# Block-sparse attention with a gated feed-forward: the second batch's value sums taken head couple by head couple, and another order of the opening

## The chip, the cores and the metric

The program runs on one core of one Trainium2 chip. The metric is the device time of one execution in microseconds (us), the median of several. The core has five engines that follow queues of their own and meet at semaphores: PE (matrix products, with PEld, its weight loads, beside it), DVE (vector operations), ACT (activations and copies), POOL (elementwise work on SBUF) and SP, which only issues DMAs.

## The reference, cut to what matters

Four batches of 8 heads, 768 positions, head size 64. Each position attends to its neighbours at a distance under 16 and to 24 summaries of blocks of 32 keys; the result feeds two large products with a piecewise gate between them.

```python
k_sum = k.reshape(B, H, nb, block, D).max(axis=3)
v_sum = v.reshape(B, H, nb, block, D).mean(axis=3)
scores_l = scale * np.matmul(q, k.transpose(0, 1, 3, 2))      # kept where |i-j| < 16
scores_s = scale * np.einsum('bhsd,bhnd->bhsn', q, k_sum) + np.log(block)
a = softmax(concat(masked scores_l, scores_s))
x = np.matmul(a, concat(v, v_sum))                            # (B*S, H*D)
h = x @ w_in
g = np.where(h >= 1, h, np.where(h <= -1, 0.0, (h + 1) ** 2 / 4))
out = g @ w_out
```

## The kernel before

The 3072 positions are worked in eight chunks `c` of 384, two to a batch, and the heads of a chunk in four couples `p`, 128 partitions each. Every piece of work is a **step**, named by a letter and its indices in hexadecimal; a step issues all its instructions on one engine, and the dictionary `steps` names its function.

Attention of a couple, with its engine: `r` load the raw keys, `k` and `q` load windowed keys and queries, `y` load the raw values, `v` load the value windows (all SP); `R` block maxima of keys (DVE), `K`, `C` put windows and maxima in place (POOL); `S` scores (PE), `M` mask and row maximum (DVE), `E` exponentials, `i` a guard on the sums (ACT), `D` reciprocals (DVE), `N0`, `N1` normalise the two heads (POOL), `T0`, `T1` transpose them (PE), `P0`, `P1` copy them out (ACT, or DVE where `P_DVE` lists them). For the value sums: `Y` sums blocks of 32 values (DVE, L256) into the tile `vsum`, `Z` transposes the sums on PE into `vs_ps` (L273 or L275), `V` scales them by 1/32 on ACT into `mean`, `W` spreads `mean` over the rows of the value tile (POOL, L284). `A` is the product with the values (PE, L358), `X` and `L` split its result into a high and a low part.

The feed-forward: `F` c f k is a quarter of the first product (three matmuls into the tile `h`), `G H I J O` the gate and the split of its result (ACT, ACT, DVE, ACT, POOL), `B` c f nine matmuls of the second product into `acc`; `U` copies `acc` to an output tile and `o` stores it. The weights come in sixteen pairs of 1 MB: `w` loads pair i (even ones of `w_in`, odd ones of `w_out`), `a`, `b` scale its words (ACT), `c` i 0 to 5 join them (DVE), `d` rounds to the high half (POOL where `HI_POOL` lists the pair, else ACT), `e` takes the rest (POOL, L186).

Order. `OPENING` is a table of 544 steps for chunk 0, most of the attention of chunk 1, all conversions of weights and the start of the feed-forward of chunk 1; in it every engine runs its steps in the order of the table. After it only PE's order is written by hand: for each chunk `c` from 1 a loop over sixteen `f` does two columns of `F` with their gates, `meet` does `A X L` of one couple of the next chunk and starts the next couple through its scores and norms, `turn` finishes a couple up to its transposes, and then come the `B` of two columns before. The other engines get those steps in an order that a scheduler sets at build time. For chunk 2, the first of batch 1, `y20`..`y23` and `Y20`..`Y23` stand at the end of the opening, and `turn(2, 0)` runs one `Z20 V20` for all four couples: one transpose of the whole `vsum` tile, 128 x 128. Chunk 0 does it couple by couple.

Raw keys, raw values, joined weights and output tiles share three buffers (tag `w` of the pool `stage`, `W_BUFS = 3`): a load into one waits until the tile that had it three allocations before is read or stored.

```python
    def turn(c, p):
        s = f"{c}{p}"
        if c % NHALF == 0 and p == 0:
            do(f"Z{s} V{s}")
        do(f"W{s} T{s}0 P{s}0 T{s}1 P{s}1")
...
        do(OPENING)
        do(" ".join(f"y{NHALF}{p} Y{NHALF}{p}" for p in range(NPAIR)))
```

Of the kernel before, what the change touches and what calls it, by code (L numbers as in the profile page):

```python
# [40 lines left out]
OPENING = """
r00 R00 K00 C00 q00 S00 m h M00 E000 E001 i00 y00 r03 R03 r01 q03 w0 g r02 K03 C03 K01 Y00 R01 q01 D00 a0 b0 S03 Z00
M03 R02 v00 V00 w2 y01 C01 N000 T000 P000 N001 T001 P001 c01 c00 y03 E031 S01 q02 W00 K02 E030 i03 c02 M01 A00 X00
D03 c03 c04 c05 N030 T030 v03 v01 a2 C02 N031 E010 E011 k10 w1 P030 Y03 T031 L00 Z03 S02 d0 e0 q10 Y01 y02 n i01
P031 M02 b2 Z01 c20 v02 k12 w4 V03 V01 E021 C10 E020 D01 W03 q12 w8 w3 F000 w6 F010 N010 N011 A03 c22 T010 k11 X03
W01 c21 c23 c24 i02 T011 S10 D02 L03 c25 P010 N021 Y02 t N020 M10 T021 P011 b1 a1 A01 w5 k13 q11 v10 Z02 P021 V02
X01 L01 c10 w7 w9 c11 T020 P020 d2 W02 A02 E100 X02 c12 L02 c14 b4 a4 C12 e2 F011 F001 F002 F003 c13 c15 d1 e1 F012
F013 c41 c40 G00 H00 S12 I00 c42 q20 wa wd k20 wc G01 H01 wb I01 r20 F030 F031 F020 F021 E101 J00 F032 i10 O00 c44
c43 J01 b3 F022 F033 D10 c45 O01 N101 a3 F023 B00 M12 d4 N100 e4 G03 G02 c30 c31 c32 c33 c34 c35 H03 b6 T100 B01 H02
P100 a6 I03 I02 F050 c60 a5 J02 b5 c61 d3 e3 c62 c63 F040 J03 a8 b8 F051 c64 F041 c50 c65 c51 F052 F042 F053 F043  # L50
O02 O03 B02 c52 d6 e6 T101 G04 H04 c53 c54 a7 I04 G05 J04 H05 B03 E121 c55 c80 I05 c82 P101 b7 c81 F070 F060 c84 J05
d5 c83 F071 c70 b9 aa F061 F072 O04 e5 F062 c85 c72 c71 c74 c73 c75 F073 F063 G06 ba C11 W10 O05 H06 B04 S11 G07 I06
M11 d8 e8 A10 d7 H07 I07 ca0 ca2 ca1 ca4 E120 B05 F090 F080 F091 ca3 J07 bc i12 D12 F081 J06 ca5 a9 e7 O06 F092 ac
O07 F082 X10 c90 L10 F093 F083 G09 da B06 G08 N120 H08 H09 c92 c91 I09 I08 c93 ea N121 E111 c94 c95 ab T120 cc0 cc2
cc1 cc4 B07 q13 F0b0 F0a0 J09 P120 F0b1 J08 cc3 cc5 d9 we wf F0a1 E110 bb F0b2 F0a2 O09 F0b3 F0a3 T121 O08 e9 v13
v12 W12 G0b i11 cb0 D11 N110 dc ec P121 B08 T110 cb2 cb4 cb1 cb3 af G0a H0b A12 B09 H0a be R20 I0a cb5 P110 ae I0b
db eb F0c0 F0d0 ce1 F0c1 F0d1 F0c2 F0d2 F0c3 X12 bf ad L12 ce0 ce2 J0a O0a ce4 ce3 ce5 F0d3 J0b O0b C13 N111 bd B0a
v11 G0d de T111 W11 cd0 cd2 G0c H0c cd1 H0d cd3 P111 ee cd4 cd5 B0b A11 S13 I0c I0d M13 J0d cf0 cf1 cf3 cf2 dd C20
ed F0e0 F0f0 F0e1 J0c O0c O0d E131 E130 cf4 F0f1 F0e2 F0f2 F0e3 G0e i13 B0c F0f3 D13 N131 W13 N130 H0e I0e J0e O0e
F110 B0d cf5 G0f H0f X11 L11 I0f T130 F100 F111 F101 T131 F102 df ef J0f P130 B0e P131 A13 X13 O0f L13 B0f U01 U02  # L60
o02 o01 U00 o00 F112 F103 F113
"""
# [16 lines left out]
def fused_kernel(ctx: ExitStack, tc: tile.TileContext, q2, kT, kwin, vT, vwin, w_in, w_out, mask, ident, out):
# [187 lines left out]
    def turn_vals(c, p):  # L267


        if f"{c}{p}" not in HALF:  # L270
            vs_pss[c, p] = ps.tile([P, 512], F32, tag="ps", name=f"vs_ps{c}_{p}")
        if c == 0:
            nc.tensor.transpose(vs_pss[c, p][:NSUM, P:2 * P], vsum[:, p, :NSUM], ident_sb)  # L273
        else:
            nc.tensor.transpose(vs_pss[c, p][:, :P], vsum.rearrange("p a b -> p (a b)"), ident_sb)  # L275
# [70 lines left out]
    def turned(c, p, j):  # L346
        pts[c, p, j] = att.tile([P, T], F32, tag=f"pt{j}", name=f"pt{c}_{p}_{j}", bufs=1)
        if f"{c}{p}{j}" in P_DVE:
            nc.vector.tensor_copy(out=pts[c, p, j][:KA], in_=t_pss[c, p, j][:KA, :T])
# [259 lines left out]
```

## Time and profile before

| what | value |
|---|---|
| median of 3 runs (lowest to highest) | 648.8 us (647.68 to 649.06) |
| the profiled execution: its own time, its span | 648.22 us, 646.4 us |
| mean granted PE clock | 0.995 |
| busy: PE, PEld, DVE, ACT, POOL | 621.3, 551.8, 244.5, 357.0, 267.8 us |
| DMA read, written | 65.00 MB, 6.29 MB |

The span runs from the first to the last instruction; 1.8 us of the time lie around it. A timeline row gives start, length, engine, line, operation and tiles, how many instructions are merged in it, and in brackets the idle time of the engine before it with what ended it. Matmuls are pipelined, so their printed lengths overlap; what a run of them takes is read from start to start.

### The profile page before, as it was taken

The numbers are of one execution on the slowest core, as the hardware profiler recorded it, in microseconds if no ns is written. First come the engines' busy times: TensorE is split into PE (matmuls) and PEld (weight loads), VectorE is DVE, ScalarE is ACT, GpSimd is POOL, SyncE is SP. The second block draws the span as 40 slices with busy tenths as digits, with TensorE's granted clock in tenths as the row PEclk, the third lists the DMA queues.
The fourth block names the chain that finished last, engine by engine and source line by source line (L and its number), as shares of the span: only waits on it lengthen the run. The fifth ranks groups of instructions, "written<-read, shape, count | busy, mean of one in ns | idle before, by whom it ended". The sixth has DMA issues, their size and how long they took to land.

```text
span 646.4 us, 11580 instructions
## 1 busy us (share of the span) xinstructions
PE 621.3 (96%) x4423; PEld 551.8 (85%) x4423; DVE 244.5 (38%) x462; ACT 357.0 (55%) x953; POOL 267.8 (41%) x307
## 2 busy tenths in 40 slices
PE   3899999599999999999999999999999999999997
PEld 2678988588989988988998898899889899889996
DVE  6999985532224322241223522143222222221111
ACT  4999984545446545545545554564554555443332
POOL 3889996252333333243334233334423333322221
PEclk9999999899999999999999999999999999999999
DMA  9999602822206322240223620152222110000001
GB/s 332 412 414 410 237 26 78 273 86 73 69 12 210 97 74 73 73 167 29 73 73 114 202 71 29 46 194 73 73 73 68 61 44 19 2 17 33 1 1 49
DMA packets 28167, 72.04 MB, mean 111 GB/s; under 512 B 2800, under 2 KB 3056, under 8 KB 28112
## 3 DMA queue, kind: packets, MB, share of 16 engines
q1 hardware_dynamic: 28112, 71.30, 31.3%
q8 instruction: 35, 0.57, 0.4%
q14 instruction: 20, 0.16, 0.1%
HBM read 65.00 MB, written 6.29 MB: 110 GB/s over the span
## 4 chain that ended last, share of the span: by engine, by line
PE 92%; DMA 3%; ACT 1%; POOL 1%; DVE 1%; SPq 1%; issue 0%; POOLq 0%
PE h L395 41%; PE acc L436 41%; PE o_ps L358 4%; PE s_ps L300 3%; PE t_ps L344 3%; DMA raw<-in_w_in 1%; DMA vraw<-in_vT 1%; DVE c L150 0%; POOL halves L186 0%; ACT pt L351 0%; ACT raw L142 0%; ACT raw L132 0%; DVE vsum L256 0%; POOL e L339 0%; SPq L209 0%
## 5 line engine op out<-in xcount | busy, mean ns | idle before, releaser
L395 PE MATMUL h<-xhi,halves 128*128 128x384 f32 x1024 | 276.2, 340 | 2.2 <-DVE t L413 1.7
L436 PE MATMUL acc<-halves,ghi 128*128 128x512 f32 x768 | 237.9, 391 | 0.0
L423 POOL TENSOR_TENSOR glo<-t,ghi 128x384 fp32r<-128x384 f32 x128 | 129.4, 1016 | 208.7 <-PE acc L436 190.6
L395 PEld LDWEIGHTS h<-xhi,halves 128*128 128x128 f32 x1024 | 186.4, 188 | 8.9 <-issue 3.6
L395 PE MATMUL h<-xlo,halves 128*128 128x384 f32 x512 | 172.4, 337 | 0.1
L436 PEld LDWEIGHTS acc<-halves,ghi 128*128 128x128 f32 x768 | 144.7, 189 | 28.6
L436 PE MATMUL acc<-halves,glo 128*128 128x512 f32 x384 | 153.5, 400 | 0.0
L413 DVE SCALAR_TENSOR_TENSOR t<-h,t 128x384 f32<-128x384 f32 x128 | 71.0, 557 | 213.9 <-ACT t L407 211.9
L401 ACT ACTIVATE t<-h,small 128x384 f32<-128x384 f32 x128 | 73.3, 574 | 87.8 <-PE h L395 87.1
L326 ACT ACTIVATE e<-e,den 128x120 f32<-128x120 f32 x192 | 73.3, 383 | 57.9 <-DVE den L315 57.9
L395 PEld LDWEIGHTS h<-xlo,halves 128*128 128x128 f32 x512 | 96.5, 189 | 1.7 <-DVE xlo L381 0.4
L418 ACT CAST ghi<-t 128x384 fp32r<-128x384 f32 x128 | 65.1, 511 | 58.7 <-DVE t L413 39.2
L436 PEld LDWEIGHTS acc<-halves,glo 128*128 128x128 f32 x384 | 72.4, 189 | 13.4 <-POOL glo L423 0.6
L407 ACT ACTIVATE t<-t 128x384 f32<-128x384 f32 x128 | 66.6, 524 | 2.1
L339 POOL TENSOR_TENSOR e<-e,den 128x360 f32<-128x360 f32 x64 | 49.5, 790 | 43.9 <-DVE den L335 43.2
L284 POOL COPY v<-mean 24x768 f32<-24x768 f32 x30 | 24.7, 823 | 78.9 <-DMA v<-in_vwin 54.5
L381 DVE TENSOR_TENSOR xlo<-o_ps,xhi 128x384 fp32r<-128x384 f32 x32 | 17.8, 555 | 86.5 <-ACT xhi L376 86.4
L376 ACT CAST xhi<-o_ps 128x384 fp32r<-128x384 f32 x30 | 14.4, 480 | 60.4 <-PE o_ps L358 60.4
L186 POOL TENSOR_TENSOR halves<-w,halves 128x1024 fp32r<-128x1024 f32 x16 | 38.6, 2418 | 0.6
L326 ACT ACTIVATION_READ_ACCUMULATOR e<-e,den 128x1 f32 x192 | 35.9, 187 | 0.0
L358 PEld LDWEIGHTS o_ps<-pt,v 120*64 120x64 f32 x720 | 24.0, 140 | 10.3 <-issue 8.8
L311 DVE SCALAR_TENSOR_TENSOR e<-s_ps,mask_sb 128x360 f32<-128x360 f32 x64 | 30.9, 524 | 4.8 <-PE s_ps L300 4.8
(61 smaller groups left out, 402.7 us busy)
## 6 DMA issues: line engine op xcount, KB each, us to landing
v<-in_vwin SPq DMA_DIRECT2D x29, 384.0 KB, 3.2
q<-in_q SPq DMA_DIRECT2D x28, 384.0 KB, 4.4
k<-in_kwin SPq DMA_DIRECT2D x28, 360.0 KB, 4.9
raw<-in_w_in SPq DMA_DIRECT2D x8, 1024.0 KB, 10.0
raw<-in_w_out SPq DMA_DIRECT2D x8, 1024.0 KB, 13.2
out<-o SPq DMA_DIRECT2D x24, 256.0 KB, 2.1
kraw<-in_kT SPq DMA_DIRECT2D x13, 384.0 KB, 3.8
vraw<-in_vT SPq DMA_DIRECT2D x13, 384.0 KB, 3.9
```

Source lines behind the costliest of these rows:

```text
L186: nc.gpsimd.tensor_tensor(out=lo, in0=converting[i].bitcast(F32), in1=hi.bitcast(F32), op=ALU.subtract)
L311: nc.vector.scalar_tensor_tensor(out=e, in0=es[c, p, j], scalar=1.0 / math.sqrt(D), in1=mask_sb[:, at:at + NT], op0=ALU.mult, op1=ALU.add)
L326: nc.scalar.activation(out=es[c, p, j][:, t, :], in_=s[:, t, :], func=AF.Exp, bias=nm[:, t:t + 1], scale=scale, accum_out=den[:, t:t + 1])
L339: nc.gpsimd.tensor_tensor(out=e, in0=e, in1=den.unsqueeze(2).broadcast_to([P, NT, KA]), op=ALU.mult)
L358: nc.tensor.matmul(o_pss[c, p][j * D:(j + 1) * D, cols], v_ts[c, p][:KA, blk, j * D:(j + 1) * D], pts[c, p, j][:KA, cols], start=True, sto ...
L395: nc.tensor.matmul(hs[c, f][:, :T], w[:, k], x, start=(k == 0 and n == 0), stop=(k == NK - 1 and n == len(products) - 1))
L401: nc.scalar.activation(out=ts[c, f], in_=hs[c, f][:, :T], func=AF.Relu, bias=ones_half, scale=0.5)
L407: nc.scalar.square(out=ts[c, f], in_=ts[c, f])
L413: nc.vector.scalar_tensor_tensor(out=g, in0=hs[c, f][:, :T], scalar=1.0, in1=ts[c, f], op0=ALU.max, op1=ALU.min)
L418: nc.scalar.copy(out=hi, in_=ts[c, f])
L423: nc.gpsimd.tensor_tensor(out=lo, in0=ts[c, f], in1=hi.bitcast(F32), op=ALU.subtract)
L436: nc.tensor.matmul(acc[c][i], a[:, rows], w, start=(f == 0 and n == 0), stop=(f == NF - 1 and n == len(products) - 1))
```

## The change

The opening's 544 steps stay the same set and get another order, a few of them another engine. Among much else, `S11`, which stood behind `B04`, now stands with `S12` ahead of the `F` steps of the second weight pair; the conversion of pair 4 starts ahead of that of pair 1 and of pair 2; and the couples of chunk 0 come in the order 0, 1, 2, 3 instead of 0, 3, 1, 2. The sums of batch 1's values (chunk 2) are no longer issued at the opening's end: `y2p`, `Y2p` come with the couple they belong to, and each couple has its own `Z2p V2p`, on 24 columns instead of the whole tile.

```diff
 OPENING = """
-r00 R00 K00 C00 q00 S00 m h M00 E000 E001 i00 y00 r03 R03 r01 q03 w0 g r02 K03 C03 K01 Y00 R01 q01 D00 a0 b0 S03 Z00
...
+r00 R00 K00 C00 q00 r01 R01 S00 m h M00 E001 E000 K01 g C01 q01 r03 i00 w0 y00 r02 K03 S01 b0 a0 R03 q02 M01 D00
...
-P_DVE = "130".split()
-X_DVE = "10 11".split()
+P_DVE = "110 120 121 131".split()
+X_DVE = "11 13".split()
...
-HI_POOL = [0, 1, 2, 3, 4, 5, 6, 8, 10, 11, 12, 13]
+HI_POOL = [0, 1, 2, 3, 4, 5, 6, 8, 9, 10, 14, 15]
...
     def turn_vals(c, p):
...
-        if c == 0:
+        if c <= NHALF:
             nc.tensor.transpose(vs_pss[c, p][:NSUM, P:2 * P], vsum[:, p, :NSUM], ident_sb)
...
     def mean_vals(c, p):
-        if c == 0:
+        if c <= NHALF:
             nc.scalar.mul(out=mean[p * SB:p * SB + NSUM], in_=vs_pss[c, p][:NSUM, P:2 * P], mul=1.0 / SB)
...
     def heads(c, p):
...
-                f"v{s} ")
+                f"y{s} v{s} Y{s} " if c == NHALF else f"v{s} ")
...
     def turn(c, p):
...
-        if c % NHALF == 0 and p == 0:
+        if c == NHALF or c % NHALF == 0 and p == 0:
             do(f"Z{s} V{s}")
...
         do(OPENING)
-        do(" ".join(f"y{NHALF}{p} Y{NHALF}{p}" for p in range(NPAIR)))
```

What this does to the queues is shown at three places. First SP, where the opening ends. Before, its rows from the stores of chunk 0's output (`out<-o_2`, and so on) to the raw values of the four couples (`vraw_0` to `vraw_3`, the steps `y20` to `y23`) and the first raw keys of that batch (`kraw_1`):

```order
L448 DMA out<-o_2_1450 128x512
L448 DMA out<-o_1_1448 128x512
L448 DMA out<-o_0_1454 128x512
L220 DMA q_2_1786<-in_q 128x768
L228 DMA vraw_0_1466<-in_vT 128x768
L228 DMA vraw_1_1469<-in_vT 128x768
L228 DMA vraw_2_1472<-in_vT 128x768
L215 DMA k_3_1975<-in_kwin 128x720
L228 DMA vraw_3_1475<-in_vT 128x768
L209 DMA kraw_1_1588<-in_kT 128x768
```

The same place on SP in the changed kernel:

```order
L448 DMA out<-o_2_1459 128x512
L448 DMA out<-o_0_1461 128x512
L448 DMA out<-o_1_1457 128x512
L220 DMA q_2_1783<-in_q 128x768
L228 DMA vraw_0_1500<-in_vT 128x768
L209 DMA kraw_1_1579<-in_kT 128x768
L228 DMA vraw_1_1656<-in_vT 128x768
L215 DMA k_3_1978<-in_kwin 128x720
L209 DMA kraw_2_1779<-in_kT 128x768
L228 DMA vraw_2_1853<-in_vT 128x768
L209 DMA kraw_3_1976<-in_kT 128x768
L228 DMA vraw_3_2050<-in_vT 128x768
```

The first couple's raw values keep their place behind the stores; the others now alternate with the raw keys, and the store of `o_1`, whose buffer `vraw_0` takes over, is the last of the three instead of the second.

Second DVE, at the sums themselves (`vsum<-vraw_p` is `Y2p`, `ksum<-kraw_p` is `R2p`, `den` the reciprocals `D20`, `t_1` to `t_3` the gates `I11` to `I13`). Before:

```order
L413 SCALAR_TENSOR_TENSOR t_1_1522<-h_1_1359,t_1_1522 128x384
L256 TENSOR_REDUCE vsum<-vraw_0_1466 128x24
L335 RECIPROCAL den_0_1495<-den_0_1495 128x6
L256 TENSOR_REDUCE vsum<-vraw_1_1469 128x24
L413 SCALAR_TENSOR_TENSOR t_2_1543<-h_2_1530,t_2_1543 128x384
L256 TENSOR_REDUCE vsum<-vraw_2_1472 128x24
L413 SCALAR_TENSOR_TENSOR t_3_1564<-h_3_1551,t_3_1564 128x384
L256 TENSOR_REDUCE vsum<-vraw_3_1475 128x24
L248 TENSOR_REDUCE ksum<-kraw_1_1588 128x24
```

The same place in the changed kernel:

```order
L413 SCALAR_TENSOR_TENSOR t_1_1513<-h_1_1360,t_1_1513 128x384
L256 TENSOR_REDUCE vsum<-vraw_0_1500 128x24
L335 RECIPROCAL den_0_1483<-den_0_1483 128x6
L248 TENSOR_REDUCE ksum<-kraw_1_1579 128x24
L413 SCALAR_TENSOR_TENSOR t_2_1534<-h_2_1521,t_2_1534 128x384
L413 SCALAR_TENSOR_TENSOR t_3_1555<-h_3_1542,t_3_1555 128x384
L256 TENSOR_REDUCE vsum<-vraw_1_1656 128x24
L248 TENSOR_REDUCE ksum<-kraw_2_1779 128x24
L256 TENSOR_REDUCE vsum<-vraw_2_1853 128x24
```

`Y20` keeps its place, with the reciprocals `D20` right behind it; `Y21` and the later sums stand behind the gates now, and PE's `Z20` waits for `Y20` alone.

Third DVE at the end of its conversions, from the last joins of weight pair 15 (`w_1320<-raw`, the step `cf5`). Before:

```order
L165 ISA w_1320<-raw_1050,c_0_1288 128x1024
L335 RECIPROCAL den_3_1278<-den_3_1278 128x6
L413 SCALAR_TENSOR_TENSOR t_14_1334<-h_14_1298,t_14_1334 128x384
L165 ISA w_1320<-raw_1050,c_1_1290 128x1024
L374 CAST xhi_1_1376<-o_ps_1_1249 128x384
```

The same place in the changed kernel:

```order
L349 COPY pt_1_0_1316<-t_ps_1_0_1237 120x384
L165 ISA w_1320<-raw_1170,c_0_1296 128x1024
L153 SCALAR_TENSOR_TENSOR c_1_1298<-raw_1170,c_1_1298 128x512
L165 ISA w_1320<-raw_1170,c_1_1298 128x1024
L413 SCALAR_TENSOR_TENSOR t_14_1343<-h_14_1284,t_14_1343 128x384
```

The gate `I0e` (`t_14`) stood ahead of the last join and now stands behind it. Ahead of that join DVE now has three copies `P110`, `P120`, `P121` more, and `X10` and `I0e` less. On POOL the step `df` of this pair is new, and it stands behind `O0e` there, the rest of the gate whose minimum is `I0e`.

More of the change, by code (lines that the diff above doesn't have):

```diff
@@ L41 @@
 OPENING = """
-r00 R00 K00 C00 q00 S00 m h M00 E000 E001 i00 y00 r03 R03 r01 q03 w0 g r02 K03 C03 K01 Y00 R01 q01 D00 a0 b0 S03 Z00
[L43 to L61, printed above, removed]
+r00 R00 K00 C00 q00 r01 R01 S00 m h M00 E001 E000 K01 g C01 q01 r03 i00 w0 y00 r02 K03 S01 b0 a0 R03 q02 M01 D00
@@ new lines @@
+N001 T001 P001 Y00 R02 Z00 E011 E010 N000 C03 T000 P000 i01 K02 C02 S02 c01 c00 c02 c04 c03 V00 w4 v00 b4 W00 q03
+D01 y02 a4 M02 c05 N011 N010 d0 e0 E021 E020 y01 w2 c40 Y02 y03 v01 k10 v02 w1 A00 T010 P010 Y01 c42 c44 T011 P011
+i02 X00 D02 S03 L00 M03 q10 N020 N021 b2 n Z01 V01 Z02 a2 V02 F010 T021 T020 Y03 Z03 W01 C10 c20 E030 F000 V03 W02
+E031 c41 c21 A01 i03 c22 c23 v03 D03 N031 P021 P020 X01 k11 k12 v10 c24 A02 S10 N030 q12 q11 c43 c25 L01 T031 t d2
+b1 T030 F001 w3 a1 X02 P030 P031 W03 M10 E101 A03 F011 X03 C11 e2 L02 c10 c45 C12 E100 i10 L03 F002 F012 F003 F013
@@ new lines @@
+w6 d4 G00 G01 H00 c11 c12 S11 D10 N101 S12 w8 w5 c14 c13 N100 I00 H01 T101 W10 w7 c15 I01 J00 F020 q13 T100 d1 k13
+v12 wa wb w9 wc q20 F021 b3 P100 F030 O00 P101 M11 k20 r20 M12 a3 c31 F022 e1 F031 c30 c33 c32 c34 c35 F023 A10 wd
+we F032 B00 F033 J01 O01 a6 G02 E120 H02 b6 I02 G03 H03 B01 e4 c60 b5 a5 J02 I03 J03 F040 c62 F050 d3 e3 F041 F051
+X10 O02 b8 c61 c63 c64 F042 c50 c65 F052 c52 c51 c54 a8 F043 B02 F053 G04 a7 O03 c53 c55 H04 d6 e6 G05 H05 B03 d5 e5
+I04 c80 I05 F060 b7 c81 c82 J05 L10 c83 c84 J04 aa E121 c70 c85 c72 c71 ba F070 i12 a9 c74 c73 c75 D12 F061 F071 O04
@@ new lines @@
+F062 F072 F063 B04 O05 d8 e8 G06 F073 G07 H06 I06 H07 B05 I07 ca0 ca2 ca1 ca4 ca3 ca5 F080 F090 F081 d7 N121 N120
+T120 F091 P120 J06 F082 F092 J07 b9 e7 O06 F083 F093 T121 W12 da E110 E111 i11 G08 O07 ac H08 c90 c92 P121 c94 c91
+I08 B06 A12 ea B07 c93 bc D11 X12 G09 H09 c95 d9 J08 O08 e9 bb F0a0 cc1 ab I09 cc0 L12 cc2 F0b0 cc3 J09 cc4 cc5 cb0
+cb1 F0a1 ae cb3 cb2 cb4 F0b1 F0a2 F0b2 F0a3 F0b3 B08 O09 N111 T111 B09 dc G0a H0a G0b H0b be ec C13 I0a cb5 J0a P111
+I0b v13 ce0 ce1 ce2 ce4 ce3 ce5 db N110 J0b v11 wf F0d0 ad bd F0c0 O0a F0d1 bf F0c1 F0d2 eb S13 F0c2 F0d3 F0c3 R20
@@ L62 @@
+O0b B0a M13 G0d T110 G0c H0d I0d cd0 C20 de ee W13 B0b H0c E130 E131 i13 F0f0 cd1 I0c J0c cd2 cd3 cd4 cd5 F0e0 F0f1
+F0e1 af D13 cf0 cf1 cf2 F0f2 F0e2 F0f3 F0e3 O0c W11 N131 P110 dd cf4 cf3 A11 T131 J0d G0e H0e ed B0c O0d N130 cf5
+I0e F110 G0f J0e H0f T130 X11 B0d P131 P130 I0f O0e F100 L11 df ef A13 J0f F111 F101 B0e F102 O0f B0f F112 X13 L13
+F103 F113 U01 U02 U00 o02 o00 o01
 """
```

## The prediction

> **What bounds the kernel now.** I read the page's busy line first, then PE's waits, then the windows, then the timeline around the one long wait.
>
> ```profile
> span 646.4 us, 11580 instructions
> PE 621.3 (96%) x4423; PEld 551.8 (85%) x4423; DVE 244.5 (38%) x462; ACT 357.0 (55%) x953; POOL 267.8 (41%) x307
> ...
> PE vs_ps L275 <- DVE vsum L256: 5.8, 1, 5.8
> PE s_ps L300 <- POOL k L251: 5.1, 1, 5.1
> PE s_ps L300 <- DMA first<-in_q: 4.1, 2, 3.9
> ```
>
> PE is busy for 621.3 of 646.4 us, so 25.1 us of it are idle. The waits (total, times, longest) name three single waits that make up 14.8 of these: two at the very start, for the first keys and queries, and one of 5.8 us on `vs_ps`, which is `Z20`, the step that the change splits. Nothing that the change adds can be hidden on PE; what it takes off PE's waits is gained in full.
>
> ```profile
> 16.00:28.50 12.50, 10.47 (x106) 7.78 (x100) 11.72 (x23) 11.71 (x48) 10.26 (x15) 1.00 1.04 413
> 28.60:40.00 11.40, 9.38 (x129) 7.45 (x128) 10.81 (x22) 11.16 (x27) 8.41 (x10) 1.00 1.04 409
> 40.00:96.00 56.00, 56.00 (x365) 49.00 (x363) 54.74 (x98) 53.36 (x101) 55.17 (x44) 1.00 0.66 258
> 120.80:124.10 3.30, 0.99 (x6) 0.67 (x4) 2.12 (x4) 2.57 (x8) 2.49 (x3) 1.00 0.97 340
> 124.20:127.60 3.40, 0.00 (x0) 0.01 (x1) 2.65 (x5) 0.51 (x1) 0.00 (x0) 0.50 0.73 218
> 127.60:130.90 3.30, 3.28 (x12) 2.91 (x13) 1.77 (x2) 1.24 (x3) 2.22 (x4) 0.50 0.56 188
> ```
>
> Columns: the stretch and its length, busy time of PE, PEld, DVE, ACT, POOL, the granted clock, the DMA share, GB/s. Two things are to be seen. From 40 to 96 us PE, DVE (54.74 of 56), ACT and POOL are all full: the opening has no slack engine. And PE's wait costs more than its length: the clock falls to 0.50 while PE is idle (124.2 to 127.6) and stays there for the first 3.3 us after it.
>
> **The wait that goes.**
>
> ```profile
> 115.34 0.85 PE L300 MATMUL s_ps<-k,q 64*64 64x120 f32 x24
> ...
> 121.46 0.34 PE L395 MATMUL h<-xhi,halves 128*128 128x384 f32 x1
> 127.62 0.44 PE L275 MATMUL vs_ps<-ident_sb,vsum 128*128 128x128 f32 x1 [5.82 <-DVE vsum L256]
> 127.86 1.49 PE L344 MATMUL t_ps<-ident_sb,e 128*120 128x128 f32 x6
> 128.99 0.78 PE L436 MATMUL acc<-halves,glo 128*128 128x512 f32 x1
> ...
> 131.38 0.40 PE L436 MATMUL acc<-halves,glo 128*128 128x512 f32 x1
> ...
> 134.24 0.92 PE L358 MATMUL o_ps<-pt,v 120*64 120x64 f32 x24
> ```
>
> PE ends `F13` at 121.63 (121.80 by its printed length), waits for all four sums, and runs `Z20`, `T200`, `T201` and the eighteen matmuls of `B10`, `B11` until `A20` starts at 134.24. The last twelve of the eighteen, at full clock again, take 134.24 - 131.38 = 2.86 us, 0.24 each; all eighteen would take 4.3 us, where they took 5.25. Now the same stretch with `Z20` waiting for `Y20` alone:
>
> ```profile
> 114.50 1.33 SPq L448 DMA_DIRECT2D out<-o  x3
> 116.28 0.34 SPq L220 DMA_DIRECT2D q<-in_q  x1
> 117.10 1.29 SPq L228 DMA_DIRECT2D vraw<-in_vT  x3
> ...
> 121.80 0.33 SPq L228 DMA_DIRECT2D vraw<-in_vT  x1
> ...
> DMA to landing us min/median/max: 3.1/3.9/5.9
> ...
> 120.82 0.95 DVE L256 TENSOR_REDUCE vsum<-vraw 128x24 f32<-128x768 f32 x1 [1.44 <-DMA vraw<-in_vT]
> 121.69 0.18 DVE L335 RECIPROCAL den<-den 128x6 f32<-128x6 f32 x1
> ...
> 126.52 0.95 DVE L256 TENSOR_REDUCE vsum<-vraw 128x24 f32<-128x768 f32 x1 [0.75 <-DMA vraw<-in_vT]
> ...
> 122.33 1.53 POOL L339 TENSOR_TENSOR e<-e,den 128x360 f32<-128x360 f32 x2
> ```
>
> The fourth load had to wait for the first sum to free its buffer (121.80), so its own sum ended at 127.5 and released PE. The first sum ended at 121.77 already. In the changed order the store of `o_1` is third instead of second, one issue of about 0.45 us later (1.33 us for three), so I put `vraw_0` at 117.55, its landing 3.7 us later as now (120.82 - 117.10), `Y20` at 121.3 to 122.2 and `Z20` at 122.4. That is not yet the end: `D20` stands behind `Y20` on DVE, so the two norms on POOL, 122.33 to 123.86 now, move to about 122.7 to 124.2, and `T201` needs the second. What is late next is therefore this norm: `T201` ends at about 124.4, and with 4.3 us for `B10`, `B11` at full clock `A20` starts at 128.7. **Gain: 134.24 - 128.7 = 5.5 us.** PE still waits some 2.2 us between 121.6 and 124.2, broken by `Z20` and `T200`.
>
> What is behind this wait elsewhere: on DVE `R21` now stands ahead of `I12` and `I13`, and waits for the raw keys issued right after `vraw_0`; that is a landing of 3.9 us from about 118, 122, then 0.95 us. PE wants their results only after `A20`, past 128, so it is covered by 4.3 us of `B` matmuls. If that load took the longest landing shown (5.9), there would still be 3 us left. `Z21` to `Z23` come four columns of `F` and `B` later each, after sums that stand some rows behind `Y20` on DVE; `W2p` now follows `Z2p` within one turn, but a turn's 4.3 us of `B` matmuls lie between it and the `A` that reads it. I cost these at nothing.
>
> **What the split adds on PE:** three transposes on 24 columns.
>
> ```profile
> L273 PE MATMUL vs_ps<-ident_sb,vsum x4: 280/370/386, 13.3 to 31.4; 128*24 128x128 f32 x4
> ```
>
> The quickest took 0.28 us; pipelined between neighbours it takes less, not under nothing. Three of them lie between 0 and 0.85 us; I take 0.4. The scaling steps are small ACT work beside an ACT that is half idle there.
>
> **The new opening.** The set of steps is the same, so PE, ACT and POOL have the same work but for the moved copies; what can change is idle time. At the start DVE has the same rows ahead of its first join in both orders: four block maxima of keys, the masks of two couples, one sum of values, one set of reciprocals.
>
> ```profile
> 14.11 0.95 DVE L248 TENSOR_REDUCE ksum<-first 128x24 f32<-128x768 f32 x1 [0.24 <-DMA first<-in_kT]
> 14.98 1.28 DVE L150 TENSOR_SCALAR c<-raw 128x512 int32<-128x512 int32 x2
> ```
>
> The last of them, `R02`, waits for the tenth load in both tables (row 14.11), so the joins start at 15 us in both. From there on DVE is full (11.72 of 12.5 us, 10.81 of 11.4, 54.74 of 56), and what it joins by a given time depends on the rows put between. The table has `S11` ahead of the second pair's `F` steps now and had it behind `B04`, which gives PE one couple's scores (0.85 us) more to do early; against that, pair 4 is joined ahead of pair 1. I take the start at nothing, within 1.5 us either way. At the end there is a term:
>
> ```profile
> 102.83 0.68 DVE L165 CUSTOM_DVE_ANT_0 w<-raw,c 128x1024 uint16<-128x1024 uint16 x1
> ...
> 104.68 0.56 DVE L413 SCALAR_TENSOR_TENSOR t<-h,t 128x384 f32<-128x384 f32 x1
> ...
> 106.29 0.56 DVE L349 COPY pt<-t_ps 120x384 f32<-120x384 f32 x1 [1.05 <-PE t_ps L344]
> ...
> 104.48 1.03 ACT L176 CAST halves<-w 128x1024 fp32r<-128x1024 f32 x1
> 105.42 0.51 ACT L418 CAST ghi<-t 128x384 fp32r<-128x384 f32 x1
> ...
> 105.67 2.39 POOL L186 TENSOR_TENSOR halves<-w,halves 128x1024 fp32r<-128x1024 f32 x1
> 108.02 1.01 POOL L423 TENSOR_TENSOR glo<-t,ghi 128x384 fp32r<-128x384 f32 x1
> ...
> 108.51 0.39 PE L436 MATMUL acc<-halves,glo 128*128 128x512 f32 x1
> ```
>
> The last join ends at 103.51, `df` runs on ACT, `ef` ends on POOL at 108.06, 4.55 us after the join, and PE starts `B0e` at 108.51, without a wait but with only 0.45 us to spare. In the new order the join has one row of 0.56 us more ahead of it (three copies in, `X10` and `I0e` out), and behind it the chain is `I0e` 0.5, its high part on ACT 0.5, `O0e` 1.0, then `df` on POOL 1.05 and `ef` 2.4, with hand-overs 5.8 us. So `ef` ends 0.56 + 5.8 - 4.55 = 1.8 us later, against a slack of 0.45 and, behind `B0e`, `F102` (0.5 us) in place of `A13`, which is 0.4 us less still to do. Cost of the opening: 1.8 - 0.45 - 0.4 = 0.95, say **0.9 us**, if DVE comes there as full as before. From below: -2 us, if the earlier attention keeps PE fuller (PE's idle time from 28.6 to 40 us is 2.0). From above: +3.5, the same again on two more weight pairs, where no engine has slack.
>
> **Sum**, against the profiled execution's 648.22 us: 648.2 - 5.5 + 0.4 + 0.9 = **644.0 us**. That execution lies 0.6 under the median of the three, inside their range, so I take no correction.
>
> [...]
>
> **Rivals.**
> 1. *The opening gains.* With more scores done early, PE gets its `F` and `B` without the small waits of the opening, and the tail term is hidden. For it: the extra couple's scores (0.85 us by the row at 115.34). Against: DVE, full from 16 to 96 us, has no less work. Time 648.2 - 5.5 + 0.4 - 2 = 641.
> 2. *The opening loses more,* 3.5 instead of 0.9: pair 4 is converted before pairs 1 and 3 now, so the first `B` may wait for pair 1. 646.6.
> 3. *The clock falls all the same,* or `vraw_0` lands as late as 5.9 us: the wait lasts to about 126.3, or half clock for some 6 us, as now from 124.2 to 130.9, costs `B` 2.5 to 3 us. With the late landing `A20` starts at 126.3 + 4.3 = 130.6, a gain of 3.6; with half clock the gain is about 2.7. 648.2 - 2.7 + 0.4 + 0.9 = 646.8, or 645.9.
> 4. *Slower:* the clock comes late in the opening. PE's first work is in short bursts; before, it ran at about half speed up to there, which the clock column does not print but the lengths show:
>
> ```profile
> 26.48 1.55 PE L358 MATMUL o_ps<-pt,first 120*64 120x64 f32 x24
> ```
>
> These 24 value matmuls took 1.55 us, the like ones at 134.24 0.92. If the new order leaves gaps between 25 and 40 us, half speed lasts until about 40; PE's 9.4 busy us from 28.6 to 40 would take up to 9 more, less the 2 us of idle there. 644 + 7 = 651. It turns the sign if half speed lasts beyond about 35 us, where half of that is lost. Against it: the same conversions feed PE's first products, at the same time.
> 5. *The split does not act:* `Z20` still waits for a later sum because all four share one tile. Chunk 0 already works that way and its transposes did not wait for later sums. 649.
>
> **How the numbers follow.** Chances: forecast 0.50 (643 to 645.5), rival 1 0.20, rival 2 0.11, rival 3 0.10, rival 4 0.06, rival 5 0.03. The range 640.5 to 647.5 leaves out rivals 4 and 5 and the ends of the others. A change under 0.2% (1.3 us) can hardly be told from none here. Faster by more: the forecast, rival 1 and most of 2 and 3, 0.86; within 0.2%: the rest of these and rival 5, 0.08; slower: 0.06.
>
> **What would show it.** Right: no wait on `vs_ps` over 1 us; after `F13` a wait of about 2 us in all that ends with POOL's norm; clock 1.00 there; `A20` 13 to 14 us after `S20` starts (18.9 now); `S20` itself at about 116. Wrong: a clock of 0.50 after 30 us; `S20` past 118.5 or before 114; `B0e` without a wait for pair 15 (then the 0.9 was wrong); idle time of PE at `Z21` to `Z23`.

## The result, and the profile after

| | median | lowest to highest | runs |
|---|---|---|---|
| before | 648.51 us | 647.68 to 649.06 | 4 |
| after | 643.33 us | 643.05 to 644.87 | 4 |

The ratio is 0.9926, with an interval of 0.9906 to 0.9946: 5.2 us faster, and the slowest run of after lies below the fastest of before. The profiled execution of after is its slowest, 644.87 us with a span of 643.1; 3.3 us less than the 646.4 of before.

The page's head of the changed kernel:

```profile
span 643.1 us, 11595 instructions
PE 620.2 (96%) x4426; PEld 551.0 (86%) x4426; DVE 245.2 (38%) x465; ACT 356.4 (55%) x953; POOL 267.2 (42%) x307
```

Its PE waits (total, times, longest):

```profile
PE s_ps L300 <- POOL k L251: 7.4, 2, 5.1
PE t_ps L344 <- POOL e L339: 4.2, 4, 3.1
PE o_ps L358 <- issue: 2.4, 2, 1.4
PE o_ps L358 <- POOL v L284: 1.9, 1, 1.9
PE vs_ps L273 <- DVE den L335: 1.0, 1, 1.0
```

The wait of 5.8 us on `vs_ps` is gone; one of 1.0 is left. New in the list is a wait of the value products, `o_ps`, that ends with no releaser ("issue"): it lies in the opening. The timeline of the changed kernel where the split acts:

```profile
116.91 0.85 PE L300 MATMUL s_ps<-k,q 64*64 64x120 f32 x24
...
118.34 0.39 SPq L228 DMA_DIRECT2D vraw<-in_vT  x1
...
123.30 0.95 DVE L256 TENSOR_REDUCE vsum<-vraw 128x24 f32<-128x768 f32 x1 [2.35 <-DMA vraw<-in_vT]
124.43 1.53 POOL L339 TENSOR_TENSOR e<-e,den 128x360 f32<-128x360 f32 x2 [0.48 <-DVE den L335]
...
124.40 0.27 PE L273 MATMUL vs_ps<-ident_sb,vsum 128*24 128x128 f32 x1 [1.05 <-DVE den L335]
125.28 0.54 PE L344 MATMUL t_ps<-ident_sb,e 128*120 128x128 f32 x3 [0.60 <-POOL e L339]
126.02 0.54 PE L344 MATMUL t_ps<-ident_sb,e 128*120 128x128 f32 x3 [0.20 <-POOL e L339]
126.32 0.48 PE L436 MATMUL acc<-halves,glo 128*128 128x512 f32 x1
130.61 0.92 PE L358 MATMUL o_ps<-pt,v 120*64 120x64 f32 x24
```

`Z20` goes as soon as its own couple's sum is there (its row names the reciprocals `den`, which run right behind that sum on DVE). PE waits 1.05 us for it, and then 0.60 and 0.20 us for POOL's two norms, as forecast: 1.85 us in all. From `S20` to `A20` it is 130.61 - 116.91 = 13.7 us, where before had 134.24 - 115.34 = 18.9: **the split gains 5.2 us**. From `A20` to the end of the span it is 643.1 - 130.61 = 512.5, where before had 646.4 - 134.24 = 512.2: **the three transposes more cost 0.3**, all of it busy time of PE (508.9 us against 508.5). And `S20` starts 116.91 - 115.34 = **1.6 us later: that much is lost in the opening**, in this execution. 5.2 - 0.3 - 1.6 = 3.3, the whole difference of the spans.

Where the opening loses it in this execution, three stretches up to the start of `S20` show, of before and then of after (the first number behind the length is PE's busy time):

```profile
0.00:20.00 20.00, 8.01 (x104) 6.38 (x105) 13.52 (x28) 10.91 (x34) 8.94 (x31) 1.00 0.93 348
20.00:45.00 25.00, 22.38 (x219) 18.12 (x219) 23.67 (x46) 23.93 (x69) 20.95 (x23) 1.00 1.04 412
45.00:115.34 70.34, 70.34 (x476) 61.13 (x474) 59.41 (x105) 57.78 (x117) 62.24 (x50) 1.00 0.53 198
```

```profile
0.00:20.00 20.00, 7.18 (x97) 5.53 (x99) 14.23 (x28) 11.62 (x35) 8.91 (x31) 1.00 0.93 350
20.00:45.00 25.00, 21.48 (x243) 17.34 (x240) 22.23 (x43) 21.37 (x65) 19.11 (x22) 0.86 0.98 376
45.00:116.91 71.91, 71.91 (x464) 63.28 (x462) 61.29 (x110) 58.44 (x116) 63.90 (x49) 1.00 0.54 205
```

From 45 us to `S20` PE is never idle in either (70.34 of 70.34, 71.91 of 71.91). So nothing that DVE or POOL do late in the opening sets `S20`: its start is PE's busy time up to there plus PE's idle time in the first 45 us. Before had 14.6 us of idle there (11.99 and 2.62), after 16.3 (12.82 and 3.52). The busy time is 100.7 and 100.6. The clock column of after shows 0.86 from 20 to 45: half clock came back, 0.50 from 28.7 to 35.6 us.

The forecast had its 0.9 us somewhere else, on pair 15 at the end of the conversions. The timeline of after there (`ef` on POOL, `B0e` on PE):

```profile
102.54 0.69 DVE L165 CUSTOM_DVE_ANT_0 w<-raw,c 128x1024 uint16<-128x1024 uint16 x1
...
107.11 2.38 POOL L186 TENSOR_TENSOR halves<-w,halves 128x1024 fp32r<-128x1024 f32 x1
...
110.60 0.39 PE L436 MATMUL acc<-halves,glo 128*128 128x512 f32 x1
```

`ef` ends at 109.49, 1.4 us later than before, and `B0e` starts at 110.60 without a wait, because PE itself came later. The slack, 0.45 us before, is 1.1 now.

### The profile page after: what moved, and what is told of

Its sections match the earlier page's. It is cut to its first block, busy times and chain, and to the rows that moved or that the text cites. A ratio compares the mean times of both kernels' runs of the same rounds, so it can differ in the third digit from the quotient of the medians.

```text
span 643.1 us, 11595 instructions
## 1 busy us (share of the span) xinstructions
PE 620.2 (96%) x4426; PEld 551.0 (86%) x4426; DVE 245.2 (38%) x465; ACT 356.4 (55%) x953; POOL 267.2 (42%) x307
## 4 chain that ended last, share of the span: by engine, by line
PE 93%; DMA 4%; ACT 1%; issue 1%; POOL 1%; DVE 0%; SPq 0%; POOLq 0%; DVEq 0%
PE h L395 41%; PE acc L436 41%; PE o_ps L358 4%; PE s_ps L300 3%; PE t_ps L344 3%; DMA v<-in_vwin 2%; DMA first<-in_q 1%; DMA first<-in_kT 1%; ACT e L326 0%; POOL e L339 0%; ACT o L444 0%; ACT t L401 0%; POOL glo L423 0%; DVE e L311 0%; POOL v L284 0%
## 5 line engine op out<-in xcount | busy, mean ns | idle before, releaser
L344 PE MATMUL t_ps<-ident_sb,e 128*120 128x128 f32 x192 | 29.3, 286 | 4.2 <-POOL e L339 4.2
## 6 DMA issues: line engine op xcount, KB each, us to landing
raw<-in_w_in SPq DMA_DIRECT2D x8, 1024.0 KB, 11.3
```

The source lines that it names most:

```text
L344: nc.tensor.transpose(t_pss[c, p, j][:KA, t * P:(t + 1) * P], es[c, p, j][:, t, :], ident_sb)
```

## The experiments

Eleven more runs were made, in three sets (e1 to e4, e5 to e8, e9 to e11), each set on a chip of its own beside the kernel before. So medians are compared within a set, and across sets the ratios, which are taken to before on the same chip. All of them, with the marks from their profiled executions (starts of the rows of `S20` and `A20` in the timeline, and spans; `idle` is PE's idle time up to `S20`, the start of `S20` less PE's busy time from 0 up to it):

| kernel | median us | ratio [interval] | `S20` | `idle` | `S20` to `A20` | `A20` to end |
|---|---|---|---|---|---|---|
| before | | | 115.34 | 14.6 | 18.9 | 512.2 |
| after | 643.33 | 0.9926 [0.9906, 0.9946] | 116.91 | 16.3 | 13.7 | 512.5 |
| e1 split only | 643.22 | 0.9914 [0.9900, 0.9927] | 116.67 | 15.7 | 15.1 | 512.5 |
| e2 order only | 647.80 | 0.9997 [0.9983, 1.0010] | 114.40 | 15.9 | 19.1 | 512.2 |
| e3 after again | 642.54 | 0.9912 [0.9899, 0.9924] | 116.82 | 17.0 | 13.2 | 512.5 |
| e4 split, `B10` first | 641.01 | 0.9885 [0.9872, 0.9899] | 114.79 | 14.6 | 12.1 | 512.5 |
| e5 opening kept busy | 644.92 | 0.9951 [0.9932, 0.9971] | 115.95 | 14.7 | 15.0 | 512.5 |
| e6 busy from the start | 645.71 | 0.9961 [0.9946, 0.9976] | 117.64 | 9.1 | 13.2 | 512.9 |
| e7 after, `B10` first | 641.37 | 0.9895 [0.9876, 0.9914] | 116.33 | 16.4 | 11.3 | 512.4 |
| e8 e6 and `B10` first | 644.23 | 0.9933 [0.9920, 0.9947] | 118.69 | 9.2 | 11.3 | 512.8 |
| e9 `q11` behind `w3` | 643.99 | 0.9946 [0.9929, 0.9962] | 116.29 | 16.7 | 13.2 | 512.5 |
| e10 `q11` behind `w6` | 647.96 | 1.0003 [0.9987, 1.0019] | 120.09 | 21.1 | 13.2 | 512.4 |
| e11 e9 and `B10` first | 642.11 | 0.9911 [0.9897, 0.9925] | 116.37 | 18.6 | 11.3 | 512.5 |

The last column is the same to 0.8 us in all: what a kernel gains or loses is decided before `A20`. The column shows the price of the three transposes: 512.2 for the two kernels without them, 512.4 or 512.5 for nine with them; why e6 and e8 have another 0.3 to 0.4 is not known.

### The two halves of the change, one at a time: e1, e2, e3

e1 keeps the old opening with its three tables and has the split; e2 has the new opening with its tables and the old sums; e3 is the changed kernel once more.

```diff
 # e1: before, with
-        if c == 0:
+        if c <= NHALF:
...
-                f"v{s} ")
+                f"y{s} v{s} Y{s} " if c == NHALF else f"v{s} ")
...
-        if c % NHALF == 0 and p == 0:
+        if c == NHALF or c % NHALF == 0 and p == 0:
...
-        do(" ".join(f"y{NHALF}{p} Y{NHALF}{p}" for p in range(NPAIR)))
 # e2: before, with OPENING, P_DVE, X_DVE and HI_POOL of the changed kernel
```

> The split of the value sums alone, with the opening's order and tables of the kernel before. Theory (the split is the whole gain, the new opening costs about 1.6 us): S20 starts at 115.3 as before, A20 13.3 to 13.8 us after it, no half clock after 40 us, span 641.2 to 642, median 5 us under the kernel before or a little more. Rival (the new opening gains too, and only the profiled execution shows it late): S20 the same, but the median is above that of the changed kernel.

> The new opening alone, with the four sums at its end and one Z20 for all as before. Theory: S20 at 116.9 as in the changed kernel, the wait on vs_ps back with some 5.8 us and half clock behind it, span 647.5 to 648.5, median 0 to 2 us above the kernel before. Rival (the new opening is worth something): median 1 us or more under the kernel before.

> The changed kernel unchanged, profiled and timed once more. [...] Rival (the half clock from 28.7 to 35.6 us belongs to this order): the same stretch within 0.5 us, S20 within 0.3 us of 116.9.

The split alone gives 0.9914, the order alone 0.9997, both together 0.9912. **The split is the whole gain; the order is worth nothing that can be measured** (an interval of -1.1 to +0.6 us). The two kernels with `B10` below agree: 0.9885 with the old order, 0.9895 with the new one, with intervals that overlap.

Two expectations failed here, both on `S20`: e1 was to have it at 115.3 and has it at 116.67, e2 at 116.9 and has it at 114.40. Over all executions of the table whose opening is untouched, `S20` lies at 114.79 to 116.67 us with the old order (before, e1, e4) and at 114.40 to 116.91 with the new one (after, e2, e3, e7). So the 1.6 us between before and after is no more than one order shows against itself, and can't be put down to the order. e3, the same kernel as after, has half clock from 31.7 to 35.1 us only, and `S20` at 116.82 all the same.

The profiled execution of e1 shows the price that the third rival named. Its timeline, and two windows of it:

```profile
116.67 0.85 PE L300 MATMUL s_ps<-k,q 64*64 64x120 f32 x24
123.94 0.27 PE L273 MATMUL vs_ps<-ident_sb,vsum 128*24 128x128 f32 x1 [0.83 <-DVE den L335]
124.81 0.54 PE L344 MATMUL t_ps<-ident_sb,e 128*120 128x128 f32 x3 [0.60 <-POOL e L339]
125.56 0.54 PE L344 MATMUL t_ps<-ident_sb,e 128*120 128x128 f32 x3 [0.20 <-POOL e L339]
131.75 0.92 PE L358 MATMUL o_ps<-pt,v 120*64 120x64 f32 x24
```

```profile
122.99:126.40 3.41, 1.78 (x11) 1.16 (x11) 3.30 (x6) 2.87 (x8) 3.09 (x5) 1.00 0.88 304
126.40:129.81 3.41, 3.41 (x10) 2.63 (x9) 1.27 (x2) 0.48 (x2) 1.16 (x2) 0.50 0.69 228
```

The same short waits as in after, and yet half clock for 3.41 us right behind them: `A20` is 15.1 us behind `S20` instead of 13.2 to 13.7. So with what is left of the wait the clock falls in some executions (0.50 from 126.40 to 129.81 here) and not in others (1.00 from 124.32 to 127.73 in after).

### What is left of the wait: `B10` first (e4, e7)

`B10` needs nothing of couple 0 of chunk 2 and stands behind its turn. Put ahead of it, its nine matmuls run while DVE and POOL finish the sum and the norms. e4 is e1 with this line, e7 the changed kernel with it.

```diff
                 if c == 1 and f + 1 in LATE:
                     do(f"j{f + 1:x} d{f + 1:x} e{f + 1:x}")
+                if c == 1 and f == 2:
+                    do("B10")
                 if f % 4 == 2 and c + 1 < NCH:
                     turn(c + 1, f // 4)
```

> The split alone (first run of this set) and on PE the nine matmuls of B10 ahead of Z20, T200, T201 instead of behind them. Theory (what is left of the wait is for the second norm, so work put ahead covers it): PE idles under 0.7 us between F13 and A20 where the changed kernel has 2.4 us, A20 11.7 to 12.2 us after S20, span 639.4 to 640.4, 1.5 to 2 us under the first run of this set. Rival (the norm, the high part of the next gate or the copies out wait on something that moves along): A20 stays 13 us or more after S20 and the span stays within 0.5 us of the first run's.

> The changed kernel with its own opening, and B10 ahead of Z20, T200, T201. Theory: as with the old opening, A20 11.7 to 12.3 us after S20, so 1.5 us less than the changed kernel's 13.2 to 13.7, median 640.7 to 641.8. Rival (the gain seen with the old opening was a lucky clock): median within 0.6 us of the changed kernel's.

The timeline of e4, and a window of it:

```profile
114.79 0.84 PE L300 MATMUL s_ps<-k,q 64*64 64x120 f32 x24
123.11 0.27 PE L273 MATMUL vs_ps<-ident_sb,vsum 128*24 128x128 f32 x1
123.22 0.82 PE L344 MATMUL t_ps<-ident_sb,e 128*120 128x128 f32 x6
126.88 0.92 PE L358 MATMUL o_ps<-pt,v 120*64 120x64 f32 x24 [0.79 <-POOL v L284]
```

```profile
120.00:124.00 4.00, 4.00 (x25) 3.54 (x24) 2.16 (x4) 2.82 (x8) 2.60 (x4) 1.00 0.92 335
```

No wait on `vs_ps` or on the norms; PE is busy for all of 4 us, and the clock stays at 1.00. `A20` now waits 0.8 us for couple 0's values (the cover behind the transposes is nine matmuls shorter). `S20` to `A20` is 12.1 us in e4 and 11.3 in e7, where after and e3 have 13.7 and 13.2. The median of e4 is 2.2 us below that of e1 beside it. e7 ran in another set than e3 and after: by the ratios it is 1.1 and 2.0 us faster, and the intervals overlap a little. The two later pairs run side by side say the same as the first: e8 is 1.5 us below e6, e11 1.9 below e9. **e4 has the lowest ratio of the study, and its interval ends where that of the change beside it (e3) begins**; from e7 it can't be told.

### Is it the clock that the opening loses by? e5, e6, e8

The profiled executions of after, e3 and e7 show half clock once more between 28 and 37 us, that of e2 doesn't. The row of the same 24 value products and the windows there, first in after, then in e2:

```profile
29.43 1.55 PE L358 MATMUL o_ps<-pt,v 120*64 120x64 f32 x24 [1.44 <-issue]
```

```profile
25.33:28.74 3.41, 1.82 (x11) 1.14 (x10) 2.94 (x6) 3.31 (x9) 1.51 (x4) 1.00 1.03 419
28.60:40.00 11.40, 9.39 (x117) 8.35 (x118) 9.29 (x19) 9.74 (x33) 8.32 (x10) 0.70 0.90 334
```

```profile
28.00 0.92 PE L358 MATMUL o_ps<-pt,v 120*64 120x64 f32 x24
```

```profile
28.60:40.00 11.40, 9.40 (x160) 8.06 (x157) 11.17 (x23) 10.60 (x32) 9.69 (x13) 1.00 1.03 405
```

e2 does 160 products in the stretch in which after does 117. So the theory was that half clock, set off by PE's gaps, costs the 2.5 us between the two in `S20`. e5 fills the gaps: `T020` is repeated twice behind `T020`, five times behind `F000`, four times behind `A01`, into the same tile. e6 also fills the first 19 us with products of zeros; e8 is e6 with `B10` first. They do work that the kernel doesn't need.

```diff
+    def again(c, p, j, place, times):
+        for _ in range(times):
+            for t in range(NT):
+                nc.tensor.transpose(t_pss[c, p, j][:KA, t * P:(t + 1) * P], es[c, p, j][:, t, :], ident_sb)
...
 OPENING = """
-... T021 T020 Y03 ... E030 F000 V03 ... c21 A01 i03 ...
+... T021 T020 p02012 Y03 ... E030 F000 p02025 V03 ... c21 A01 p02034 i03 ...
```

> The changed kernel with PE's gaps between 26.6 and 31.3 us filled: the transposes T020 are repeated once behind themselves, five times behind F000 and four times behind A01 (same result each time). Theory (half clock between 28 and 36 us, brought on by these gaps, is what puts S20 at 116.9): clock 1.00 from the first grant on, S20 at 114.2 to 115.2, span 1.5 to 2.5 us under the changed kernel's 643.1, median 0.5 to 2 us under it. Rival (PE is late there for other reasons, the conversions): full clock, but S20 still at 116.5 to 117.

> As the run before it, and besides PE's waits of the first 19 us are filled with products of zeros (9 ahead of S00, 6 behind it, 13 behind S01, 8 behind S02) that nothing reads. Theory (PE runs at half speed until some window has been busy enough): full clock by 8 us, scores of S01 in 0.85 instead of 1.48 us, S20 1 to 2 us earlier than in the run before it, at 113 to 114. Rival (the first 25 us are set by loads and by DVE, ACT and POOL): full clock early, S20 within 0.4 us of the run before.

> All three together: filled gaps, zeros in the first 19 us, B10 ahead of Z20. Theory: the gains add, S20 at 113 to 114 and A20 12 us later, median 638.5 to 640, the fastest of all. Rival (early full clock is covered by the loads): the same as the run before it within 0.6 us.

The clock did as wanted, the time didn't. e5 has 1.00 from 28.6 us up to `S20`; in e6 the zeros run from 1.15 to 5.13 us, the 24 scores at 5.24 take 0.84 us (those of after at 5.07, behind an idle PE, 1.48), and full clock is lost only once in the opening (0.80 from 20.0 to 28.6 us). But `S20` came at 115.95 and 117.64 instead of the 115.2 or less and the 114 that were expected, and the medians 644.92 and 645.71 (0.9951 and 0.9961; e5's interval overlaps that of after, not that of e3). The table shows part of why. e5 has 1.7 us less idle than after, but its busy time up to `S20` is 115.95 - 14.65 = 101.3 against 100.6, where the same work without a fall of the clock takes 98.5 (e2: 114.40 - 15.89). The products put in cost some 2.8 us of PE themselves. Even so `S20` comes 1.0 us earlier than in after; but the profiled execution of e5 then has half clock behind `Z20` (125.5 to 128.9 us), and from `S20` to `A20` loses 1.3 us against after. That fall is not all of e5's loss: its three executions with a mean clock of 0.999 or 1.000 took 644.04 to 644.65 us, and what they lose is not traced. In e6 idle is 7 us less and busy 8 us more. **Filling the gaps with products that nobody needs bought the clock in the opening and no time.** e8, expected as the fastest of all at 638.5 to 640, also lay 2.9 us above e7.

The theory is not refuted by this, only this remedy fails: e2 and after differ by 2.1 us of busy time for the same products, and by 0.45 of idle.

### Is it the queue of loads? e9, e10, e11

In the seven runs with the new opening so far, `S20` followed the issue of the weight load `w3` with a nearly constant distance of 81.5 to 82.1 us. SP's waits in after from 24 to 46 us show what holds `w3`:

```profile
SPq L220 <- PE s_ps L300: 4.6, 2, 2.9
```

The queries of chunk 1's couple 1, `q11`, stand ahead of `w3`; they have only two buffers and wait for the scores `S10`. Meanwhile the DMA share falls to 0.90 (row 28.60 above; 1.03 in e2). The theory: the weights come late, and all behind them. e9 puts `q11` behind `w3`, e10 behind `w6`, e11 is e9 with `B10` first.

```diff
-... S10 N030 q12 q11 c43 ... F001 w3 a1 ... F013 w6 d4 ...
+... S10 N030 q12 c43 ... F001 w3 q11 a1 ... F013 w6 d4 ...       # e9
+... S10 N030 q12 c43 ... F001 w3 a1 ... F013 w6 q11 d4 ...       # e10
```

> The changed kernel with one load moved on SP: the queries of the second half's pair 1 (q11) go behind the weight load w3 instead of ahead of it. Nothing else moves. Theory (the queue of issues): a buffer of the queries comes free only when the scores S10 have run, all later weight loads stand behind q11 on SP, the DMA engines run empty for about 2 us, and everything that hangs on the weights, up to S20, comes that much later. In seven runs with this opening order S20 stood 81.5 to 82.1 us behind the issue of w3 (32.90 to 37.16), whatever the clock. Then here: w3 issued by 31 us, DMA engines at 1.0 or above between 28.6 and 40 us (0.86 to 0.93 in the runs that lost), S20 at 114.0 to 115.2, the median at 640.5 to 641.8 us, 1.0 to 2.0 under the changed kernel's 642.5 to 643.3. Rival (the clock, or the order of the products on PE, sets the opening's end and the weight loads only follow it): w3 is issued early but S20 stays at 116.4 to 117.0 and the median at 642.5 to 643.5. A second rival: q11 now lands late and S11 waits for it, S20 at 116 to 118 with a wait on the queries at S11 of over 1 us.

> The same load q11 moved further, behind w6: two weight loads stand ahead of it. By the theory of the queue one load of 1 MB covers the about 2 us in which the DMA engines ran empty, so the second gives nothing more: S20 at 114.0 to 115.4 and the median within 0.7 us of the kernel with q11 behind w3, unless q11's landing makes S11 wait (then up to 1.5 us more). If neither kernel beats the changed one by 1 us, the theory of the queue falls.

> The changed kernel with q11 behind w3 and B10 ahead of the turns. If the two gains lie in different places they add: S20 at 114.0 to 115.2, the products of pair 0 (A20) 11.0 to 12.1 us behind it, the median at 638.5 to 640.0 us (the changed kernel with B10 alone gave 641.37, before's opening with the split and B10 641.01). If the opening's gain is not real: 641.0 to 641.7.

One row of e9's windows, then the row of `S11` in e9's timeline, and the same row in e10's:

```profile
28.60:40.00 11.40, 10.01 (x121) 8.62 (x120) 9.72 (x20) 9.38 (x30) 8.62 (x11) 0.74 1.03 409
```

```profile
40.28 1.46 PE L300 MATMUL s_ps<-k,q 64*64 64x120 f32 x48 [0.48 <-DMA q<-in_q]
```

```profile
42.50 1.93 PE L300 MATMUL s_ps<-k,q 64*64 64x120 f32 x48 [4.36 <-DMA q<-in_q]
```

The DMA engines are full now (1.03), and nothing is gained: 643.99 us, a ratio of 0.9946 where after has 0.9926 and e3 0.9912. e10 loses the whole gain of the split, 647.96, and e11 stays above the 638.5 to 640.0 that were expected if the gains added, 642.11. The theory falls, and the second rival came true: `S11` waits for `q11`, 0.5 us in e9, 4.4 in e10, 1.9 in e11, and PE, with all that stands behind `S11` in its order, waits with it. The constant distance to `w3` was no cause. `w3` and `S11` both follow `S10`; and as PE is hardly idle after 45 us (0.16 us at most, in e2), `S20` follows `S11`: 76.2 us behind it in after (40.71), 76.0 in e9, 77.6 in e10, where the clock fell once more in between (0.91 from 40 to 60 us).

### What the thirteen profiles say together

`S20` is PE's busy time plus PE's idle time, and the new order changes both. Idle up to `S20` is 14.6 to 15.7 us with the old order (before, e1, e4), and 15.9 to 17.0 with the new one where nothing was added or moved (after, e2, e3, e7). Busy time is 100.2 to 101.0 with the old order. With the new one it is 98.5 in e2 and 97.8 in e11, where the clock, once full, stays so through the opening (1.00 up to `S20`, as in before, e1 and e4), and 99.8 to 100.6 in after, e3 and e7, where it falls again. So by these profiles the new order loses up to 2 us by waits, gains some 2 by doing less at half clock at the start, and loses most of these again where the clock falls: about nothing in sum, which is what e2's median says. The mean clocks of the executions don't settle it. In e3 those with 0.999 took 642.03 and 642.42 us, those with 0.997 took 642.54, 642.86 and 644.29; but in after 0.992 goes with 643.09 and 0.995 with 644.87, in e1 0.992 with 642.99 and 0.999 with 642.50 to 643.79.

Two profiles come near to a measurement. e2 and e7 run the same opening, and `A01` (the row at 28.00 above) starts at 28.00 and 28.02 us in them; e7 then has half clock from 29.9 to 36.8 us, e2 hasn't. From `A01` to `S11`, e2 first:

```profile
28.00:37.89 9.89, 7.89 (x121) 6.83 (x121) 9.66 (x20) 9.37 (x30) 8.26 (x10) 1.00 1.03 409
28.02:40.11 12.09, 10.29 (x120) 8.97 (x120) 9.98 (x21) 9.48 (x30) 8.76 (x12) 0.72 1.00 374
```

PE is busy for 2.4 us more over the same products and idle for 0.2 less, so `S11` comes 2.2 us later, and `S20` 1.9. In after, with half clock of the same length, most of it behind `A01`, the stretch takes 11.3 us (29.43 to 40.71), 1.4 more than in e2. And in e9 and e11, again one opening, 10.3 us of half clock and none lead to `S20` at 116.29 and 116.37: where `S11` waits for a load, the full clock only lengthens that wait (0.5 and 1.9 us).

The other half of the 2.8 us by which `S11` is later in after (40.71) than in e2 (37.89) has nothing to do with the clock: `A01` starts 1.43 us later, before the clock falls. On ACT, first in after, then in e2, the rows are the step `b2`, which needs the load of weight pair 2, and `V03` behind it:

```profile
24.88 1.16 ACT L142 ACTIVATE raw<-raw 128x1024 int32<-128x1024 uint32 x1 [1.40 <-DMA raw<-in_w_in]
29.07 0.26 ACT L279 ACTIVATE mean<-vs_ps 24x128 f32<-24x128 f32 x1
```

```profile
23.43 1.15 ACT L142 ACTIVATE raw<-raw 128x1024 int32<-128x1024 uint32 x1
27.64 0.27 ACT L279 ACTIVATE mean<-vs_ps 24x128 f32<-24x128 f32 x1
```

The load landed later in after, all of ACT behind it shifted by 1.4 us, and `A01` starts 0.1 us behind the end of `V03` in after, e2, e3 and e7 alike. Both use buffers of the tag `ps`, so `A01` most likely waits for the one that `V03` reads; this would be the wait that the profile lists without a releaser. e3 has the same late load (1.51), e2 and e7 haven't. Why it lands late in some executions is open.

All this compares single executions after the fact. No run here takes the fall of the clock away without adding work, so **its price in the opening, 1 to 2 us, is worked out, not shown by an experiment**.

## Why the prediction was right, and where not

- **The total.** 644.0 was forecast with a range of 640.5 to 647.5; the median is 643.33. On its own basis, one profiled execution to another, the forecast was -4.2 us and the profiles show -3.3; the medians differ by 5.2, mainly because the profiled execution of after is the slowest of four. Split and transposes alone were forecast at -5.5 + 0.4 = -5.1, which is what e1's median shows (643.22 against 648.31); the +0.9 of the opening doesn't show in the medians.
- **The split, -5.5.** Right in mechanism and nearly in size: -5.2 in after, -5.7 in e3 (18.9 - 13.2). `T201` was to end 9.1 us behind `S20`; it ended 9.7 behind it in after (126.56), 9.1 in e3. `B10` and `B11` were to take 4.3 us: 126.32 to 130.61. That the clock stays full there, behind a wait of 2.2 us, was an estimate that no run of before shows; it stayed in after (1.00 from 124.32 to 127.73, behind waits of 1.85 us in all), and didn't in e1 and e5 (rival 3). `vraw_0` was issued earlier than I had it, 1.4 us behind `S20` instead of 2.2, and took longer, 5.0 us to the start of its sum instead of 3.7. What came next was POOL's norm, as said; the wait on `vs_ps`, 1.05 us, is just over the 1 us that the prediction allowed.
- **The costs put at nothing.** PE's waits of after name no wait at `Z21` to `Z23` or behind `R21`. Right.
- **Three transposes, +0.4.** 0.3 to 0.4, by the distance from `A20` to the end, in nine of the eleven profiles that have them.
- **The opening, +0.9.** Wrong in its reason; that its size lies between what after's profile and the medians show is luck. The step that failed is "Cost of the opening: 1.8 - 0.45 - 0.4": it took the chain of pair 15 for the end of the opening. `ef` did come 1.4 us later, but `B0e` waited for nothing, the sign that the prediction itself had named for this. PE is full from 45 us on, so the opening is decided before; I had read "the joins start at 15 us in both, from there on DVE is full" as the end of the question, where PE's own idle time and clock in the first 45 us were the answer. In its place the runs show +1.6 in after, +1.5 in e3, -0.9 in e2's profile, and 0 with an interval of -1.1 to +0.6 in e2's medians.
- **Rival 3**, the clock falls all the same, at 0.10: it happened in the profiled executions of e1 and e5 (15.1 and 15.0 us from `S20` to `A20`), not in those of after, e3, e9 and e10 (13.2 to 13.7). It cost 1.3 to 1.9 us, less than the 2.8 that I gave it, since half clock lasted 3.41 us (0.50 from 126.40 to 129.81 in e1) and not twice that.
- **Rival 4**, half clock in the opening, at 0.06: it came, but for 3.4 to 6.8 us only and not up to 40. After's half clock from 28.7 to 35.6 us is also the "clock of 0.50 after 30 us" that the prediction named as a sign of being wrong: the term of the opening had no clock in it, and its reckoning of the split, 85 us later, doesn't hang on it.

## What to carry to other kernels

A wait that is split leaves a shorter one behind it; put work that is ready ahead of it, and the rest of the wait goes with it (here another 1.5 to 2.2 us for one moved step, in the three pairs run side by side; behind it the clock was 1.00 from 124 to 131 us in the profiles of e4 and e7, where e1 had 0.76). To see what sets a point in time, look for the last stretch in which the bounding engine is idle: behind it only that engine's busy time counts, and a chain on other engines, however full they are, moves nothing as long as that engine doesn't have to wait for it. A constant distance between two events in many runs is no cause; moving the first alone showed it here.

## What the runs showed of the hardware

The profiled executions show twelve falls of the granted clock, eleven of them behind a stretch that held work. The stretches of 3.41 us ahead of them held 0.00 us of PE busy time (e2), 0.82 (e10), 0.92 (the first of two in e9), 0.93 (e3), 1.04 (before), 1.43 (e8), 1.56 (e6), 1.78 (e1 and e7), 1.82 (after), 1.84 (e5) and 2.20 (the second in e9). Counted off in steps of 3.41 us from the fall in the same profile, other stretches had no fall behind them with as little: 1.64 us (e10 at 36.50), 1.69 (e2 at 28.96, 48 short products), 1.92 and 2.10 (e10 at 26.26 and 125.25). So PE's busy time alone doesn't tell whether a fall follows: here the clock fell behind 2.20 us of work and stayed behind 1.64. One row of after and one of e2, both without a fall behind them (25.33 above is one with):

```profile
120.91:124.32 3.41, 2.45 (x14) 2.03 (x12) 1.06 (x4) 2.96 (x13) 1.00 (x1) 1.00 0.95 350
```

```profile
28.96:32.37 3.41, 1.69 (x48) 1.46 (x48) 3.41 (x7) 3.38 (x8) 2.06 (x5) 1.00 1.04 408
```

In the profiled executions all stretches at half clock behind a fall lasted 3.4 us (3.41 in e1 and e5) or twice that (6.83 in e7), and one kernel has more of them in one execution than in another: 6.8 us in the opening of after (28.7 to 35.6), 3.4 in that of e3 (31.7 to 35.1); the six executions of e7 have mean clocks from 0.995 to 1.000.
